# Retention attention and an ELU feed-forward layer on one core: attention in 18 items of four 64-token chunks and eight heads, instead of 36 items of two chunks and four heads

## The chip, the cores and the metric

The kernel runs on one core of a Trainium2 chip. The metric is the time of one execution in microseconds (us) on the device; lower is better. The engines are named as in the profile: PE (TensorE), DVE (VectorE), ACT (ScalarE), POOL (GpSimd) and SP (SyncE, which issues most transfers).

## The reference: what is computed

```python
scores = scale * np.matmul(q, k.transpose(0, 1, 3, 2))      # q, k, v: 8 batches, 8 heads, 576 tokens, 64
gamma = 1.0 - 2.0 ** (-5.0 - np.arange(H, dtype=np.float32))
Dmat = np.where(rel >= 0, gamma[:, None, None] ** rel[None, :, :], 0.0)
x = np.matmul(scores * Dmat, v)                             # then heads side by side: 4608 x 512
h = x @ w_in                                                # 512 -> 2048
g = np.where(h > 0.0, h, np.exp(np.minimum(h, 0.0)) - 1.0)
out = g @ w_out                                             # 2048 -> 512
```

There is no softmax, so the decay is put into q and k beforehand, and attention over earlier tokens can go through a running 64x64 state per head (the sum of k times v) instead of through scores.

## The kernel before, in words

**The plan.** The kernel's operations are objects (`Op`, line 22) with a cost per engine, dependencies, a rank, and the buffers they take and use. `Plan.run` (line 66) goes through a modelled time and gives each engine the ready operation of lowest rank that finds its buffers free. This fixes, once and for all, the order of the instructions of every engine; the chip then runs each engine's list in that order, with waits where data or a buffer is not there yet. Buffers come from `SLOTS` (line 202): `f` are six PSUM banks for everything that PE writes, `sc` one pair of banks for the scores alone.

**Attention before.** An item (36 of them, list `ORDER`) is a main item, 256 tokens of one batch and four heads, or a tail, the last 64 tokens of two batches for eight heads. For each:

- SP loads q, k and v (`load_main`, line 349: 256 KB each; `load_tail`, line 377). POOL and DVE scale q and k into bf16 (`scaled`, line 421; instructions at line 427), POOL or ACT casts v (line 443). q and k are transposed, on PE for the first seven items (`turn_pe`, line 448), by a transposing DMA from SP afterwards (line 491).
- A main item has two chunks of 128 tokens; even and odd tokens are interleaved, so a chunk lies on 64 partitions. `do_scores` (line 547) makes 16 matmuls of 128 columns on 64x64 tiles of PE. DVE multiplies them with the causal mask (line 673, 128x1024). `do_values` (line 585) makes 16 more of 128 columns, `do_state` (line 605) 16 of 64 columns for the sums of k times v per chunk. `do_inter` (line 570) multiplies q with the running states: 128x128 weights, two matmuls of 128 columns per chunk that has a state before it.
- `after_state` (line 619) adds the sums on DVE (lines 630 to 639) and spreads each state to a block-diagonal matrix with a product with `diag` (line 647, mostly POOL). `put_x` (line 696) copies x into the tile `xt` (bf16), two copies of 128x256 per item.
- `stretch(prev, it)` (line 738) is one piece of PE's list: inter of the item before, scores of this item, values of the item before, states of this item. It takes two `f` banks. The first five items are in smaller pieces (`early`, line 772).

**FFN before.** A block is 256 tokens (18 blocks). `ffn1` (line 801) fills one bank with two groups of four matmuls of 256 columns; ACT takes exp (line 817), ACT or DVE does the middle step (lines 827 to 831), DVE joins both into g (lines 839, 841). `ffn2` (line 853) makes a 128x512 output tile with 16 matmuls of 512 columns, in runs of two or four; ACT or DVE copies it out (line 872), SP stores it (line 880). POOL issues the loads of w_in (line 406) and w_out (line 414), four of 512 KB each, at places tied to named operations (`WG`, `WOG`).

All matmuls go through the helper `mm` (line 245), so the profile gives that line for all and the tiles tell them apart: `f<-xt,w_in_sb` is FFN1, `f<-w_out_sb,g` FFN2, `sc<-qkT` scores, `f<-pt,vn` values, `f<-vn,qkn` states, `f<-qkT,s_mid` and `f<-qkT,s_end` inter.

Of the kernel before, what the change touches and what calls it, by code (L numbers as in the profile page):

```python
# [22 lines left out]
class Op:  # L23


    def __init__(self, name, cost, deps, emit, rank, take=(), use=(), banks=(), dma=None, after=None):
        self.name, self.cost, self.emit, self.rank = name, cost, emit, rank
        self.deps = [d for d in deps if d is not None]
        self.turn = [] if after is None else [after]
        self.take, self.use, self.banks, self.dma = take, [*use, *(t[1] for t in take)], banks, dma  # L30
        self.eng = self.start = self.end = self.done = None
        self.slot, self.waits = {}, []


class Plan:
# [30 lines left out]
    def run(self, began):  # L66
# [29 lines left out]
        def pick(e, now):  # L96
            best = None
            for op in ready[e]:
                if best is not None and best[0] <= op.rank:
                    continue  # L100
# [12 lines left out]
                if got is not None:  # L113
                    best = op.rank, op, got
            return best
# [5 lines left out]
        for e, t in began.items():  # L121
            heapq.heappush(events, (t, next(count), None))
        now = 0.0
# [62 lines left out]
ENTER, LEAVE = 1.25, 0.55  # L186


LEAD = 64
HOLD = {}  # L190
RANKS = {}
TOGETHER = 1
EARLY = 5
LOOSE = True
LASTB = 15
ORDER = (0, 1, 2, "t0", 3, "t1", 4, 5, 6, "t2", 7, "t3")
PE_TURN = 7
WG = ("ck11", "ck11", "ck11", "ck12")
WOG = ("ck13", "ck13", "ck13", "ck13")
# [11 lines left out]
def kernel(  # L211
# [15 lines left out]
    FT = 4  # L227
    ST = 64
    NU = FT + 1
    KJ = DM // P  # L230
    NFT = DF // P
    TB = 256
    NP = NFT // 2
    MID = S // 2
    C = 64
    assert (DM, S, D, HP) == (H * D, FT * P + ST, 64, KJ)
# [20 lines left out]
    for h in range(H):  # L257
        nc.vector.memset(lgt[:, h : h + 1], lg[h])
    pos_i = const.tile([P, NU], I32, name="pos_i")
    nc.gpsimd.iota(pos_i[:, :FT].rearrange("p (t e) -> p t e", e=2), pattern=[[2 * P, 2], [1, 2]], base=-MID,  # L260
                   channel_multiplier=2)
    nc.gpsimd.iota(pos_i[:ST, FT:], pattern=[[0, 1]], base=FT * P - MID, channel_multiplier=1)
    nc.gpsimd.iota(pos_i[ST:, FT:], pattern=[[0, 1]], base=MID - FT * P, channel_multiplier=-1)
    pos = const.tile([P, NU], FP32, name="pos")
# [5 lines left out]
    bt = const.tile([P, 1], FP32, name="bt")  # L270
    nc.vector.memset(bt[:ST], math.log(scale))
    nc.vector.memset(bt[ST:], 0.0)
    expo = const.tile([P, NU, H], FP32, name="expo")
    nc.vector.tensor_tensor(
        expo,
        pos.unsqueeze(2).to_broadcast([P, NU, H]),
        lgt.unsqueeze(1).to_broadcast([P, NU, H]),
        ALU.mult,
    )
    gq = const.tile([P, NU, H], FP32, name="gq")  # L280
    nc.scalar.activation(gq[:, :FT], expo[:, :FT], AF.Exp, bias=bq)
    nc.scalar.activation(gq[:, FT], expo[:, FT], AF.Exp, bias=bt)
    gk = const.tile([P, FT, H], FP32, name="gk")
    nc.scalar.activation(gk, expo[:, :FT], AF.Exp, bias=bk, scale=-1.0)

    mask = const.tile([P, 2, 2, C], BF16, name="mask")
    nc.vector.memset(mask, 1.0)
    for c in range(2):
        for ek in range(2):
            for eq in range(2):  # L290
                m = mask[c * C : (c + 1) * C, ek, eq]
                nc.gpsimd.affine_select(out=m, in_=m, compare_op=ALU.is_ge, fill=0.0, base=eq - ek,
                                        pattern=[[2, C]], channel_multiplier=-2)
    mask_t = const.tile([P, ST], BF16, name="mask_t")
    nc.vector.memset(mask_t, 1.0)
    for c in range(2):
        m = mask_t[c * ST : (c + 1) * ST]
        nc.gpsimd.affine_select(out=m, in_=m, compare_op=ALU.is_ge, fill=0.0, base=0, pattern=[[1, ST]],
                                channel_multiplier=-1)
    diag = const.tile([P, 2], FP32, name="diag")  # L300
    nc.gpsimd.memset(diag, 0.0)
    nc.gpsimd.memset(diag[:D, :1], 1.0)
    nc.gpsimd.memset(diag[D:, 1:], 1.0)
# [3 lines left out]

    plan = Plan(SLOTS)  # L310
# [8 lines left out]
    holds, chain = [], {}  # L319
# [4 lines left out]
    items = []  # L324
    for b in ORDER:
        for r in range(FT if isinstance(b, int) else 1):
            it = Item()
            it.tail = not isinstance(b, int)
            if it.tail:
                it.half = int(b[1]) % 2  # L330
                it.b, it.blk = 2 * int(b[1]), "AB"[int(b[1]) // 2]
            else:
                it.b, it.T, it.w = b, r // 2, r % 2
                it.blk = 2 * b + it.T
            items.append(it)
    for n, it in enumerate(items):
        it.n = n
        it.early = n < FT
    at = {(it.b, it.T, it.w): it for it in items if not it.tail}

    seq = list(range(2 * B))
    seq = [*seq[:B], "A", *seq[B:LASTB], "B", *seq[LASTB:]]
    place = {blk: i for i, blk in enumerate(seq)}
    for it in items:
        it.rank = it.n * 4 - 64 if it.early else place[it.blk] * 16 - LEAD + 6 * (it.half if it.tail else it.w)

    def load_main(it, srcs="qkv"):
        n = it.n  # L350
        if not hasattr(it, "ld"):
            it.ld = {}
        for s in srcs:
            src = {"q": q, "k": k, "v": v}[s]
            key, cls = (("rv", n), "rv") if s == "v" else (("rq" + s, n), "rqk")

            def emit(op, src=src, key=key):
                dst = tiles[key].rearrange("p h e d -> p h (e d)")
                pin(nc.sync.dma_start(
                    dst,  # L360
                    src[it.b, 4 * it.w : 4 * it.w + 4, 2 * P * it.T : 2 * P * (it.T + 1), :].rearrange(
                        "h (p e) d -> p h (e d)", e=2),
                ))

            take, use, held = [T(cls, key, [P, 4, 2, D], FP32)], [], []
            if s == "q" and n in HOLD:
                def emit_hold(op, key=key):
# [5 lines left out]
            it.ld[s] = add(f"ld{s}{n}", {"SP": 0.46}, held, emit, len(plan.ops), take=take, use=use,  # L373
                           dma=(0.9 if n or s != "v" else 1.8, 32), after=chain.get(0))
            chain[0] = it.ld[s]

    def load_tail(it):
        n = it.n
        it.ld = {}
        for j in range(2):  # L380
            for i, src in enumerate((q, k)):
                def emit(op, j=j, i=i, src=src):
                    pin(nc.sync.dma_start(tiles["rqt", n, j][i * ST : (i + 1) * ST],
                                          src[it.b + j, :, FT * P :, :].rearrange("h p d -> p h d")))

                it.ld[i, j] = add(f"ldt{i}{j}{n}", {"SP": 0.46}, [], emit, len(plan.ops),
                                  take=[T("rqt", ("rqt", n, j), [P, H, D], FP32)] if i == 0 else [],
                                  use=[] if i == 0 else [("rqt", n, j)], dma=(0.8, 32), after=chain.get(0))
                chain[0] = it.ld[i, j]
        for j in range(2):  # L390
            def emit(op, j=j):
                pin(nc.sync.dma_start(tiles["rvt", n][j * ST : (j + 1) * ST],
                                      v[it.b + j, :, FT * P :, :].rearrange("h p d -> p h d")))

            it.ld["v", j] = add(f"ldt2{j}{n}", {"SP": 0.46}, [], emit, len(plan.ops),
                                take=[T("rvt", ("rvt", n), [P, H, D], FP32)] if j == 0 else [],
                                use=[] if j == 0 else [("rvt", n)], dma=(0.8, 32), after=chain.get(0))
            chain[0] = it.ld["v", j]
# [3 lines left out]
    def load_w_in(n0, n1, after):  # L402
        c = slice(n0 * 512, n1 * 512)
# [4 lines left out]
        op = add(f"wi{n0}", {"POOL": 0.8}, [], emit, -1000, dma=(2.75 * (n1 - n0), 32 * (n1 - n0), 4.9), after=after)  # L408
        for n in range(n0, n1):
            w_in_ld[n] = op  # L410

    def load_w_out(n, after):
        def emit(op):
            pin(nc.gpsimd.dma_start(w_out_sb[:, 4 * n : 4 * n + 4],
# [6 lines left out]
    def scaled(it, i, e, cost):  # L421
# [4 lines left out]
        def emit(op):  # L426
            pin(alu[op.eng].tensor_tensor(tiles[key][:, i, e], tiles[raw][:, :, e], g, ALU.mult))  # L427
# [566 lines left out]
```

## Time and profile before

| what | value |
|---|---|
| three runs | 310.29, 311.6 (median), 312.34 us |
| profiled execution: span from first to last instruction | 307.9 us |
| what lies around the span (median less span; the profile gives no time of its own beyond the span) | 3.7 us |
| PE, DVE, ACT, POOL busy | 294.6, 218.0, 153.4, 148.3 us |
| instructions | 8903 |
| FFN1 matmuls (128x256) | 1152 |
| moved by DMA | 50.12 MB, 163 GB/s over the span |

Times in the profile are microseconds from the first instruction, and a group's line gives its engine, source line, operation, output and input tiles, shape and count. A matmul's duration runs from its start to its modelled end and overlaps its neighbours, so what it costs on PE is read from start to start. Slices are fortieths of the span. A line of waits gives the engine and tile that waited, who released it, and the total time, the number of waits and the longest one.

### The profile page before, as it was taken

How to read it: one execution, taken by the hardware profiler on the slowest of the kernel's cores; microseconds unless marked ns; L12 is line 12 of the kernel's file. 1: busy time of each engine (PE TensorE's matmuls, PEld its weight loads, DVE VectorE, ACT ScalarE, POOL GpSimd, SP SyncE). 2: the span in 40 equal slices, each digit the busy share in tenths (PEclk: the TensorE clock that was granted, in tenths of full speed). 3: DMA queues.
4: the chain of work that ended last, by engine and by line, in shares of the span. 5: the costliest groups of instructions: out<-in, count | busy, mean ns of one | idle time of the engine just before them, and what ended most of it. 6: DMA issues, size and time to landing. Idle time of an engine off the chain costs nothing.

```text
span 307.9 us, 8903 instructions
## 1 busy us (share of the span) xinstructions
PE 294.6 (96%) x3600; PEld 207.0 (67%) x3647; DVE 218.0 (71%) x395; ACT 153.4 (50%) x297; POOL 148.3 (48%) x258
## 2 busy tenths in 40 slices
PE   7789999999999999999999999999999999999995
PEld 3576747767677676676676676667776666666654
DVE  4997835887687878888778787667676666666650
ACT  3467815565556645554545545345446343444431
POOL 5983469958876779988776775003011000000000
PEclk9999999999999999999999999999999999999999
DMA  6999999999999999999999998101011010000122
GB/s 198 271 216 216 216 270 256 263 249 211 247 231 211 217 247 277 243 247 305 247 214 212 274 221 151 36 35 38 34 36 36 35 36 34 36 34 34 39 56 78
DMA packets 103768, 50.12 MB, mean 163 GB/s; under 512 B 45744, under 2 KB 99248, under 8 KB 103728
## 3 DMA queue, kind: packets, MB, share of 16 engines
q1 hardware_dynamic: 99504, 45.37, 69.9%
q0 software_dynamic: 4224, 4.19, 8.0%
q8 instruction: 28, 0.46, 0.6%
q14 instruction: 12, 0.10, 0.1%
HBM read 36.70 MB, written 9.44 MB: 150 GB/s over the span
## 4 chain that ended last, share of the span: by engine, by line
PE 86%; DMA 10%; issue 2%; DVE 1%; POOL 1%; ACT 0%
PE f L245 81%; DMA rqk<-in_q_dram 6%; DMA rqk<-in_k_dram 4%; PE sc L245 3%; PE f L455 1%; POOL qkn L427 0%; PE f L953 0%; DVE qkT L461 0%; POOL s_end L647 0%; DVE qkn L427 0%; ACT ot L872 0%; DVE s_end L647 0%; DVE zero L250 0%; DVE end L639 0%
## 5 line engine op out<-in xcount | busy, mean ns | idle before, releaser
L245 PE MATMUL f<-xt,w_in_sb 128*128 128x256 bf16 x1152 | 147.5, 273 | 0.1
L245 PE MATMUL f<-w_out_sb,g 128*128 128x512 bf16 (+1 forms) x546 | 138.0, 373 | 4.3 <-issue 3.0
L817 ACT ACTIVATE e<-f 128x512 f32<-128x512 f32 x144 | 86.0, 597 | 109.2 <-PE f L245 107.5
L245 PEld LDWEIGHTS <-w_in_sb 128*128 128x128 bf16 x1152 | 111.5, 98 | 38.0
L831 DVE TENSOR_SCALAR em<-e 128x512 bf16<-128x512 f32 x105 | 53.3, 508 | 49.9 <-ACT e L817 49.3
L245 PEld LDWEIGHTS <-g 128*128 128x128 bf16 x592 | 56.0, 98 | 39.4
L841 DVE SCALAR_TENSOR_TENSOR g<-f,em 128x512 bf16<-128x512 f32 x105 | 72.2, 688 | 9.1 <-DVE em L831 0.5
L647 POOL TENSOR_TENSOR s_mid<-mid,diag 128x256 bf16<-128x256 f32 x32 | 20.0, 624 | 51.2 <-ACT mid L630 24.6
L427 POOL TENSOR_TENSOR qkn<-rqk,gq 128x256 bf16<-128x256 f32 x61 | 37.6, 632 | 11.6 <-DMA rqk<-in_q_dram 7.6
L427 POOL TENSOR_TENSOR qkn<-rqk,gk 128x256 bf16<-128x256 f32 x59 | 38.4, 667 | 5.3 <-DMA rqk<-in_k_dram 5.1
L673 DVE TENSOR_TENSOR pt<-sc,mask 128x1024 bf16<-128x1024 f32 x32 | 38.9, 1215 | 1.7 <-PE sc L245 1.7
L839 DVE SCALAR_TENSOR_TENSOR g<-e,f 128x512 bf16<-128x512 f32 x39 | 26.1, 682 | 6.0 <-ACT f L827 6.0
L872 ACT COPY ot<-f 128x512 f32<-128x512 f32 (+1 forms) x36 | 20.6, 575 | 17.8 <-PE f L245 17.7
L708 ACT CAST xt<-f 128x256 bf16<-128x256 f32 x50 | 20.0, 450 | 10.8 <-PE f L245 10.2
L827 ACT ACTIVATE f<-f 128x512 f32<-128x512 f32 x36 | 21.4, 595 | 0.0
L443 POOL CAST vn<-rv 128x512 bf16<-128x512 f32 x28 | 17.6, 629 | 7.4 <-DMA rv<-in_v_dram 7.3
L647 POOL TENSOR_TENSOR s_end<-end,diag 128x256 bf16<-128x256 f32 x28 | 17.4, 623 | 4.2 <-DVE end L639 2.7
L245 PE MATMUL sc<-qkT 64*64 64x128 bf16 x512 | 13.4, 222 | 1.7 <-DVE qkT L461 1.6
L245 PE MATMUL f<-pt,vn 64*64 64x128 bf16 x512 | 12.7, 217 | 0.0
L245 PEld LDWEIGHTS <-qkT 64*64 64x64 bf16 x512 | 8.2, 106 | 5.4 <-DVE qkT L461 2.2
L506 POOL TENSOR_TENSOR qkt<-rqt,gq 128x256 bf16<-128x256 f32 x16 | 9.9, 638 | 3.0 <-DMA rqt<-in_k_dram 3.0
L461 DVE COPY qkT<-f 128x512 bf16<-128x512 bf16 x11 | 4.6, 421 | 9.4 <-PE f L455 9.4
(65 smaller groups left out, 139.4 us busy)
## 6 DMA issues: line engine op xcount, KB each, us to landing
rqk<-in_q_dram SPq DMA_DIRECT2D x32, 256.0 KB, 5.1
rqk<-in_k_dram SPq DMA_DIRECT2D x32, 256.0 KB, 5.2
rv<-in_v_dram SPq DMA_DIRECT2D x32, 256.0 KB, 5.0
out_dram<-ot SPq DMA_DIRECT2D x31, 256.0 KB, 3.7
w_in_sb<-in_moe_w_in_dram POOLq DMA_DIRECT2D x4, 512.0 KB, 12.6
w_out_sb<-in_moe_w_out_dram POOLq DMA_DIRECT2D x4, 512.0 KB, 19.3
out_dram<-ot SPq DMA_DIRECT2D x10, 128.0 KB, 2.4
rqt<-in_q_dram SPq DMA_DIRECT2D x8, 128.0 KB, 4.0
```

The costliest lines, as they stand in the source:

```text
L245: pin(nc.tensor.matmul(*a, **kw))
L427: pin(alu[op.eng].tensor_tensor(tiles[key][:, i, e], tiles[raw][:, :, e], g, ALU.mult))
L443: pin(copy[op.eng](tiles["vn", n], tiles["rv", n]))
L647: pin(alu[op.eng].tensor_tensor(tiles[key].rearrange("p h (j d) -> p h j d", j=2), tiles[src].unsqueeze(2).to_broadcast([P, 2, 2, D]), dia ...
L673: pin(nc.vector.tensor_tensor(tiles["pt", n].rearrange("p i h n -> p (i h) n"), tiles["sc", n].rearrange("p i (h n) -> p (i h) n", h=2), m ...
L708: pin(copy[op.eng](dst, src))
L817: pin(nc.scalar.activation(tiles[ekey], tiles[hkey], AF.Exp))
L827: pin(nc.scalar.activation(ph, ph, AF.Relu))
L831: pin(alu[op.eng].tensor_scalar_add(em, e, -1.0))
L839: pin(nc.vector.scalar_tensor_tensor(g, e, -1.0, ph, ALU.add, ALU.min))
L841: pin(nc.vector.scalar_tensor_tensor(g, ph, 0.0, tiles["em", blk, p], ALU.max, ALU.min))
L872: pin(copy[op.eng](tiles[okey][:, :width], tiles[pkey][:, :width]))
```

## The change

Attention goes in 18 items (`ATT`) of all eight heads: 16 of 256 tokens of a batch, and two of the last 64 tokens of four batches ("X", "Y"). Each has four chunks of 64 tokens, and with even and odd tokens interleaved a chunk lies on 32 partitions. Scores use 64x32 tiles of PE (64 matmuls of 64 columns an item), values and states 32x64 tiles (64 of 64 columns each), inter 128x128 weights and four matmuls of 64 columns per chunk that has a state. A state is kept per chunk: four sums on DVE or ACT, and two copies of half the partitions into a standing zeroed block-diagonal tile (`ring`) on POOL, ACT or DVE, in place of the product with `diag`. The mask is two DVE products of 128x512 per item.

PSUM is one pool of eight banks. A stretch takes six together: two for scores, four for x (columns 0 to 255) and the new states (columns 256 to 511). A test in the plan (`gate`) decides when the plan begins to collect those six banks.

FFN goes in 11 blocks: four of 256 tokens, seven of 512. For the latter FFN1's matmuls have 512 columns, four to a bank. Two items, not five, are in small pieces at the start; four, not seven, are transposed on PE; weights come in five pieces (256, 256, 512, 512, 512 KB) for w_in and four for w_out, not before given times of the plan (`AT`). The rank lead of attention over FFN (`LEAD`) is 96 for 64. In the built program PE has 1152 score, 1152 value, 1024 state and 256 inter matmuls, 64 transposes, 256 FFN1 matmuls of 256 columns and 448 of 512.

```diff
-    "f": 6, "sc": 1,
-    "rqk": 8, "rv": 8, "qkn": 5, "vn": 6, "qkT": 5, "pt": 3,
-    "rqt": 4, "rvt": 2, "qkt": 4, "vt": 2, "qkTt": 4, "ptt": 2,
-    "xt": 5, "g": 20, "e": 4, "em": 4, "ot": 5, "mid": 4, "end": 4, "s_mid": 4, "s_end": 16,
+    "f": 8, "rq": 3, "rk": 3, "rv": 3, "qkn": 3, "vn": 3, "qkT": 3, "pt": 2,
+    "xt": 4, "g": 33, "e": 4, "em": 4, "ot": 5, "S": 6,
...
-LEAD = 64
+LEAD = 96
+EARLY = 2
+PE_TURN = 4
+AT = {"wi0": 9.6, "wi1": 10.4, "wi2": 11.2, "wi3": 13.0, "wi4": 15.0, "wo0": 17.0, "wo1": 19.0, "wo2": 22.0, "wo3": 25.0}
+ATT = ((0, 0), (0, 1), (1, 0), (1, 1), (2, 0), (2, 1), (3, 0), (3, 1), (4, 0), (4, 1), "X",
+       (5, 0), (5, 1), (6, 0), (6, 1), (7, 0), (7, 1), "Y")
+FFN = (((0, 0),), ((0, 1),), ((1, 0),), ((1, 1),), ((2, 0), (2, 1)), ((3, 0), (3, 1)), ((4, 0), (4, 1)),
+       ((5, 0), (5, 1)), ((6, 0), (6, 1)), ("X", "Y"), ((7, 0), (7, 1)))
...
     def do_scores(it):
-        for hl in range(2):
-            for ek in range(2):
-                for i in range(2):
-                    r = slice(i * D, (i + 1) * D)
-                    for c in range(2):
-                        cs = slice(c * C, (c + 1) * C)
-                        o = (hl * 2 + ek) * P
-                        mm(pairs(sc[cs, i, o : o + P]), tt[r, 4 + ek * 2 + hl, cs], queries(n, r, hl, c),
-                           start=True, stop=True)
+        tt = tiles["qkT", it.n]
+        for hp in range(HP):
+            for ek in range(2):
+                for c in range(NC):
+                    for i in range(2):
+                        part = slice(i * D, (i + 1) * D)
+                        sc = tiles["sc", it.n, i].rearrange("p (h k n) -> p h k n", h=HP, k=2)
+                        mm(pairs(sc[rows(c), hp, ek]), tt[part, 1, ek, hp, rows(c)], queries(it, part, hp, c),
+                           start=True, stop=True)
...
+    def do_inter(it, xkey):
+        for c in range(NC):
+            s = state_of(it, c)
+            if s is not None:
+                for hp in range(HP):
+                    acc((xkey, c), 2, pairs(tiles[xkey, c][:, hp * C : (hp + 1) * C]), tiles[s][:, hp],
+                        queries(it, slice(0, P), hp, c))
+
+    def do_values(it, xkey):
+        vn, pt = tiles["vn", it.n], tiles["pt", it.n]
+        for hp in range(HP):
+            for ek in range(2):
+                for c in range(NC):
+                    for i in range(2):
+                        acc((xkey, c), i, tiles[xkey, c][i * D : (i + 1) * D, hp * C : (hp + 1) * C],
+                            vn[rows(c), 2 * hp + i, ek], pt[rows(c), i, hp, ek])
...
+            def emit_s(op, skey=skey, prev=prev, st_ap=st_ap):
+                if prev is None:
+                    pin(copy[op.eng](tiles[skey], st_ap()))
+                else:
+                    pin(nc.vector.tensor_tensor(tiles[skey], st_ap(), tiles[prev[1]], ALU.add))
...
+            def emit_b(op, skey=skey, bkey=bkey):
+                for i in range(2):
+                    part = slice(i * D, (i + 1) * D)
+                    pin(copy[op.eng](tiles[bkey][part, :, part], tiles[skey][part]))
...
     def stretch(prev, it):
...
+        st = add(f"A{it.n if it else 'last'}", {"PE": cost}, deps, emit, (it or prev).rank - 4, use=use)
+        reserve(st, ([("sc", it.n, i) for i in range(2)] if it else []) + banks_of(xkey))
...
     def ffn1
...
-            for f in range(2):
-                ft = 2 * p + f
+            for f, ft in enumerate(fts):
                 for j in range(KJ):
-                    mm(ph[:, f * TB : (f + 1) * TB], w_in_sb[:, j, ft * P : (ft + 1) * P], xt[:, j],
+                    mm(ph[:, f * blk.w : (f + 1) * blk.w], w_in_sb[:, j, ft * P : (ft + 1) * P], xt[:, j],
                        start=(j == 0), stop=(j == KJ - 1))
```

More of the change, by code (lines that the diff above doesn't have):

```diff
@@ L287 @@
+    nc.scalar.activation(gk, expo, AF.Exp, bias=bk, scale=-1.0)
+    mask = const.tile([P, 2, 2, R], BF16, name="mask")
     nc.vector.memset(mask, 1.0)
-    for c in range(2):
+    for c in range(NC):
         for ek in range(2):
[L290 to L303, printed above, removed]
+            m = mask[c * R : (c + 1) * R, ek]
@@ L317, in T @@
         return (cls, key, shape, dt)
-    holds, chain = [], {}
     class Item:
         pass
[L324 to L349, printed above, removed]
-        n = it.n
[L351 to L366, printed above, removed]
+    items, at = [], {}
@@ L367, in emit_hold, with load @@
+    chain, holds = {}, []
+    def load(it):
+        n = it.n
+        it.ld = {}
+        for s, src in (("q", q), ("k", k), ("v", v)):
+            key, cls = ("r" + s, n), "r" + s
+            take, use, held = [T(cls, key, [P, H, 2, D], FP32)], [], []
+            if n in HOLD and s == "q":
                 def emit_hold(op, key=key):
@@ L372, in load_main @@
                 take, use = [], [key]
[L373 to L398, printed above, removed]
@@ new lines, in prepare, with emit @@
+        for hs in halves:
+            def emit(op, hs=hs):
+                pin(copy[op.eng](tiles[vkey][:, hs], tiles["rv", n][:, hs]))
+            vfirst = not it.cv
+            it.cv.append(add(f"cv{hs.start}_{n}", {"ACT": 0.62, "POOL": 0.64, "DVE": (0.42, 0.3)} if it.early else
+                             {"POOL": 0.64, "ACT": (0.62, 1.0)}, lds(it, "v", hs), emit, it.rank,
+                             take=[T("vn", vkey, [P, H, 2, D], BF16)] if vfirst else [],
+                             use=[("rv", n)] + ([] if vfirst else [vkey]), after=None if vfirst else it.cv[0]))
@@ new lines, in rows, with queries, pairs @@
+    def rows(c):
+        return slice(c * R, (c + 1) * R)
+    def queries(it, part, hp, c):
+        return tiles["qkT", it.n][part, 0, :, hp, rows(c)]
+    def pairs(ap):
+        return ap.rearrange("p (e r) -> p e r", e=2)
+    def do_scores(it):
+        tt = tiles["qkT", it.n]
[7 more added lines that the diff above has]
+                           start=True, stop=True)
@@ L746, in stretch @@
         if it is not None:
[L747 to L751 removed]
+            deps += [*it.turned, *it.cv]
+            use += [("qkT", it.n)] + ([] if it.tail else [("qkn", it.n), ("vn", it.n)])
+            cost += cost_of(it, "s" if it.tail else "st")
         def emit(op):
@@ L853, in ffn2, with rows_of @@
-    def ffn2(blk, it, c, per, rank, n0=0, n1=DM):
-        pkey, okey = ("p", blk, it, n0), ("ot", blk, it, n0)
-        nfp, width = per // 2, n1 - n0
+                pin(nc.vector.scalar_tensor_tensor(g, ph, 0.0, tiles[mkey], ALU.max, ALU.min))
+        blk.g[p] = add(f"g_{blk.i}_{p}", {"DVE": 0.69}, [md], emit_g, rank, take=[T("g", gkey, [P, 512], BF16)],
+                       use=[hkey, ekey, mkey], banks=[(hkey, 0)])
+        return f1
+    def rows_of(blk, t):
+        it, half = blk.its[t // 2], t % 2
+        if not it.tail:
+            return [(0, P, it.b * S + it.T * TB + half * P)]
+        return [(j * C, C, (it.b + 2 * half + j) * S + 2 * TB) for j in range(2)]
```

691 lines of the change are left out of this document (316 added, 375 removed).

## The prediction, on record before the changed kernel ran

> **What bounds the kernel now.** I read the page's busy times first, then the waits of TensorE (PE) after the start, then the timeline of PE.
>
> ```profile
> PE 294.6 (96%) x3600; PEld 207.0 (67%) x3647; DVE 218.0 (71%) x395; ACT 153.4 (50%) x297; POOL 148.3 (48%) x258
> PEclk9999999999999999999999999999999999999999
> DMA  6999999999999999999999998101011010000122
> PE 86%; DMA 10%; issue 2%; DVE 1%; POOL 1%; ACT 0%
> ```
>
> PE is busy 96% of the 307.9 us at full granted clock, and the chain that ends last is PE for 86%. DMA is busy in nine tenths of every slice up to about 185 us, and 10% of the chain is DMA: that is the start. From 48 to 305 us the waits of PE are this one line:
>
> ```profile
> PE f L245 <- issue: 3.0, 19, 0.2
> ```
>
> 19 waits of 0.16 us, each in front of an "x3" of FFN2 where the code issues four: a matmul without a record. So PE never waits once the kernel runs, and the time after the start is the sum of what PE issues. What one thing costs on PE is not its mean duration (matmuls overlap) but the step from one start to the next:
>
> ```profile
> 49.81 3.66 PE L245 MATMUL f<-xt,w_in_sb 128*128 128x256 bf16 x32
> 53.31 1.03 PE L245 MATMUL f<-w_out_sb,g 128*128 128x512 bf16 x4
> 54.17 1.04 PE L245 MATMUL f<-xt,w_in_sb 128*128 128x256 bf16 x8
> ...
> 55.91 0.27 PE L245 MATMUL f<-qkT,s_end 128*128 128x128 bf16 x2
> 56.02 0.28 PE L245 MATMUL f<-qkT,s_mid 128*128 128x128 bf16 x2
> 56.22 0.42 PE L245 MATMUL sc<-qkT 64*64 64x128 bf16 x16
> 56.47 0.39 PE L245 MATMUL f<-pt,vn 64*64 64x128 bf16 x16
> 56.70 0.29 PE L245 MATMUL f<-vn,qkn 64*64 64x64 bf16 x16
> 56.92 1.05 PE L245 MATMUL f<-xt,w_in_sb 128*128 128x256 bf16 x8
> ...
> 81.10 0.32 PE L245 MATMUL sc<-qkTt 64*64 64x64 bf16 x16
> 81.25 0.40 PE L245 MATMUL f<-pt,vn 64*64 64x128 bf16 x16
> ```
>
> To be seen: 32 FFN1 matmuls of 256 columns take 53.31 - 49.81 = 3.50 us (109 ns each), four FFN2 matmuls of 512 columns 0.86 us (216 ns each). One attention stretch (states into x, scores, values, new states) takes 56.92 - 55.91 = 1.01 us: four 128-column matmuls at 56 ns, a change of tile shape, 16 + 16 + 16 small ones, a change back. Sixteen scores of 64 columns take 0.15 us. In the single records four 64x64 tiles start 3.3 ns apart and run side by side; the next four follow 56 ns later at 128 columns and 32 ns later at 64. A change of shape costs 0.09 to 0.10 us beyond the normal step (last inter start 62.31, first score 62.46; the step is 0.056).
>
> FFN needs 1152 x 0.109 + 576 x 0.216 = 250.0 us of the span whatever the attention does; the rest, 58 us, is start, attention and end (3.4 us from the last matmul to the end).
>
> **The change part by part.**
>
> Attention before: of 32 main items, 16 have four inter matmuls (1.01 us) and 16 have two (0.90 us): 30.7 us. Four tails at about 0.6 us (8 inter at 29 ns, scores 0.15, values 0.13, shape change 0.1): 2.4 us. Together 33.1 us. After: 18 items for all 8 heads. Inter: 16 matmuls of 64 columns at the 29 ns that the tails' form shows (12 for a first block). Scores, values, states: 64 matmuls each, eight tiles side by side. The trace has no 64x32 or 32x64 tile. Bounds: eight side by side at the 32 ns of a 64-column group make 8 x 0.032 = 0.25 us for 64; only four side by side, as the rows show, make 0.51 us. I take 0.25, because a tile of the new shape is half of one that the rows show and every eight consecutive matmuls name eight different tiles. There is one more shape change, since scores and values now differ. A second block: 0.46 + 0.09 + 0.25 + 0.09 + 0.25 + 0.25 + 0.10 = 1.49 us; a first one 1.38; a tail 1.24. 8 x 1.49 + 8 x 1.38 + 2 x 1.24 = 25.4 us. Term: -7.7 us.
>
> FFN1: seven of eleven blocks are 512 tokens wide, 448 matmuls at the 216 ns of the 512-column row in place of 896 at 109: 448 x (0.216 - 0.218) = -0.9 us.
>
> Start: the first FFN1 stands at 18.76 us, after w_in, whose loads are issued from 9.29 us and take 8.5 us at least for 512 KB. After, the first two pieces are 256 KB and follow POOL's four scalings, as in before; the landing is between the 5 us of a 256 KB load on SP's queue and those 8.5 us, and I take 7.5 (near its own kind), so the first FFN1 about 17.3: -1.5 us (between -4 and 0). Against it PE has 64 transposes for 56 and eight groups of them, not six, behind the first FFN1, each 0.25 us, each possibly late behind a load as they are in before (waits of 0.2 to 1.0 us there): +1.0 us (0 to +4). q, k and v of an item come as six loads of 256 KB in either kernel, so SP's queue gives the first items no earlier.
>
> PSUM banks: scores have no banks of their own any more. A stretch takes six of eight banks (two for scores, four for x and states), so FFN has two until VectorE and ScalarE have emptied them. Lower end 0, the row above. Upper end: the last FFN1 bank ahead of a stretch needs exp 0.60, relu 0.60, g 0.69 and hops, 2.2 us, while the order puts one FFN2 run of 0.86 us behind it: 1.3 us late x 16 stretches = 21 us. In the middle of the order the FFN1 bank before that has 2.6 us, and two banks may stay in use, so I stay near the lower end: +2 us.
>
> VectorE: 36 masks of 0.69 for 32 of 1.215 and four of 0.68: -16.8 us. 56 state sums of 128x256 at about 0.42 (the 128x256 copy's row) for 51 of 0.28: +9.3 us. FFN's chains are the same 144 of 512. It stays off the path, as do POOL (124 half-height block copies, 100 of them on POOL, for 64 block products of 0.62; the scalings are half as many and twice as wide) and ACT. Their cover is FFN on PE; if it is gone, POOL's 148 us over the first 190 show how little room there is: the next things late would be the block copies, and with them the inter matmuls at the head of a stretch. On SP the transposing DMAs are 28 wide for 25 wide and 8 half ones, tail loads take rows of 512 B for 256 B: 0.
>
> Sum: -7.7 - 0.9 - 1.5 + 1.0 + 2.0 = -7.1 us. The span goes from 307.9 to 300.8. The median of the three runs, 311.6, lies 3.7 us over the span, which I leave as it is: **304.5 us**, 2.3% faster.
>
> **The rivals.**
>
> Issue of small matmuls (slower). A full stretch was 52 pairs of load and matmul and becomes 208. How fast PE is fed matters only once its queue is empty: its closing drain is on record at 302.40 us with exactly 16 loads still to start, so 16 pairs are queued. The densest place of the trace has 47 loads within 457 ns from 86.25 us; less the 16 queued, 31 pairs in 457 ns, so a pair takes at most 14.7 ns. It takes at least the 3.3 ns between neighbours. Behind the inter matmuls 176 pairs must come in 0.95 us. At 14.7 ns they take 2.59 us: +1.64 us x 16 stretches = 26 us, about 331 us. The gain of 7 us is gone from 8 ns per pair on (176 x 8.1 = 1.42 us, +0.47 x 16). For it: nothing in before asked for more than 52 pairs in a row. Against it: no start in those bursts is late, up to the last group.
>
> [...]
>
> Four tiles, not eight, at once (the change does not do what it says): 0.25 us more in each of 52 groups of 64, 13 us, 317 us. For it: no such row. Against: the four tiles of before never hinder each other.
>
> Banks: 0.5 us per stretch rather than 0.13, 6 us more, 310.5 us. For it: six banks at once. Against: no bank wait in before, where a stretch held four.
>
> Loads late: the last stretch has 104 us of FFN behind it (its matmuls in the order at the steps above), in before 68 us, so attention ends 36 us earlier, about when the loads ended in before (DMA drops after 185 us). Transposing DMAs stand at least 6.2 us ahead of their scores in before and land in 4.9: 1.3 us of room. If DMA delivers no faster than its mean of 240 GB/s, a stretch late by 5 us costs 5 us, since PE's order is fixed: 309.5 us.
>
> **How the numbers follow.** Forecast, 300 to 308 us by its own bounds: 0.50. Better, through a start 5 us shorter and no bank waits (297.5): 0.07. Issue: 0.18, half of it mild (8 to 9 ns a pair, 311 to 317), half worse. The 25 ns rule: 0.02. Four tiles: 0.05. Banks: 0.11. Loads late: 0.07. Three runs of this kernel spread by 0.7%, so about 1% is what a measurement tells from no change. Faster by over 1% (below 308.5): the forecast, the better case and half of banks and loads late, 0.66. Within 1%: the other half and some mild issue, 0.14. Slower: 0.20. The range leaves out about 0.1 at each end: 298 to 317 us.
>
> **What would show it.** Right: 64 scores in a row from start to start within 0.27 us, a full stretch of 1.5 us, FFN1 at 216 ns per 512 columns, no PE wait after 50 us over 0.3 us, first FFN1 near 17 us. Wrong: 64 small matmuls taking 0.4 us or more with even steps (issue) or with groups of four (tiles); PE waits on ACT or DVE ahead of a stretch (banks) or on a transposing DMA or POOL (loads); a VectorE over 80% busy.

## The result, and the profile after

The changed kernel takes 371.51 us (median of five runs, 368.33 to 372.76): 1.191 times the kernel before, 95% interval 1.186 to 1.197. I had said 304.5 us, and 317 at most. Ratios, here and below, are from runs counted as fast (at most 1.5% above the fastest of the same kernel), against the kernel before as it ran in the same batch (medians 310.24 to 311.6 us).

The page of the changed kernel: busy time, the granted clock by slices, the queue that brings instructions, and the shares of the chain that ended last.

```profile
span 366.4 us, 11811 instructions
PE 323.2 (88%) x5066; PEld 186.4 (51%) x5097; DVE 213.4 (58%) x402; ACT 167.1 (46%) x329; POOL 142.7 (39%) x239
PEclk9788999699989989989999889699999999999999
q8 instruction: 40, 0.66, 0.8%
PE 84%; issue 11%; POOL 2%; DMA 1%; ACT 1%; DVE 1%; SPq 0%; POOLq 0%; ACTq 0%
```

PE's busy share fell from 96 to 88%, the clock is below nine tenths in a quarter of the slices (for none before), and 11% of the chain is "issue": PE stood still and nothing that the profile shows held it. The waits of PE (total, number, longest) say the same:

```profile
PE f L252 <- issue: 31.9, 26, 3.8
PE f L866 <- issue: 3.6, 1, 3.6
PE f L252 <- DVE zero L257: 1.3, 1, 1.3
```

After the start no wait on a bank, a load or a copy is over 0.8 us; 35 us are waits for nothing. The timeline of TensorE (PE) shows where:

```profile
60.53 1.03 PE L252 MATMUL f<-w_out_sb,g 128*128 128x512 bf16 x4
61.39 0.51 PE L252 MATMUL f<-qkT,bd 128*128 128x64 bf16 x12
61.84 0.68 PE L252 MATMUL f<-qkT 64*32 64x64 bf16 x64
62.45 0.70 PE L252 MATMUL f<-pt,vn 32*64 32x64 bf16 x64
62.95 0.57 PE L252 MATMUL f<-vn,qkn 32*64 32x64 bf16 x41
66.64 0.39 PE L252 MATMUL f<-vn,qkn 32*64 32x64 bf16 x23 [3.12 <-issue]
67.36 3.19 PE L252 MATMUL f<-w_out_sb,g 128*128 128x512 bf16 x7 [0.33 <-issue]
70.35 8.10 PE L252 MATMUL f<-xt,w_in_sb 128*128 128x256 bf16 x64
```

Three things are to be seen. Scores take 62.45 - 61.84 = 0.61 us up to the first value, where I had 0.34 (0.25 and a change of shape of 0.09). In the middle of the states, whose data are all there, PE stands still for 3.1 us. And the seven FFN2 matmuls behind it take 2.99 us to the next start, 427 ns each instead of 216: half the clock.

From the single records, the 58.5 us by which the span grew, by the steps between weight loads: pauses (steps over 0.6 us) 37.2 us in 15 places, for 3.4 before: +33.8; the rest of FFN 258.9 us for 245.8: +13.1, of which 51 steps of 380 to 440 ns are some 10; the rest of attention 51.1 us for 46.7: +4.4; fillers at the start 14.2 for 7.0: +7.2.

The pauses have an address. The built program has 10212 instructions on PE (7296 before), and 0.66 MB in 40 packets are 16 KB each. That makes 64.2 bytes for an instruction (62.9 in the kernel before, which has 28 packets), so I take 64, and 256 of them in a packet. Nearly all the long pauses stand where the place in PE's program is 194 or 195 modulo 256, which I take for the place between the last instruction of one packet and the first of the next: after each of the 15 PE goes on 1.1 to 1.6 us behind the end of a packet. (In the records all 15 stand 91 to 96 pairs behind a multiple of 128; the count slips because some records are missing.)

### The profile page after: what moved, and what is told of

It reads as the page before. It is cut to its first block, busy times and chain, and to the rows that moved or that the text cites. A ratio compares the mean times of both kernels' runs of the same rounds, so it can differ in the third digit from the quotient of the medians.

```text
span 366.4 us, 11811 instructions
## 1 busy us (share of the span) xinstructions
PE 323.2 (88%) x5066; PEld 186.4 (51%) x5097; DVE 213.4 (58%) x402; ACT 167.1 (46%) x329; POOL 142.7 (39%) x239
## 4 chain that ended last, share of the span: by engine, by line
PE 84%; issue 11%; POOL 2%; DMA 1%; ACT 1%; DVE 1%; SPq 0%; POOLq 0%; ACTq 0%
PE f L252 82%; DMA rk<-in_k_dram 1%; PE f L459 1%; POOL bd L582 1%; POOL qkn L427 1%; PE f L866 0%; ACT e L723 0%; DVE em L737 0%; ACT qkT L468 0%; SPq L368 0%; DVE g L747 0%; DVE g L745 0%; ACT f L733 0%; ACT S L563 0%; ACT ot L784 0%
## 5 line engine op out<-in xcount | busy, mean ns | idle before, releaser
L252 PE MATMUL f<-xt,w_in_sb 128*128 128x512 bf16 (+1 forms) x694 | 150.6, 359 | 1.8 <-ACT e L723 0.8
L252 PEld LDWEIGHTS <-w_in_sb 128*128 128x128 bf16 x704 | 71.4, 103 | 63.2 <-issue 11.0
L582 POOL CAST bd<-S 64x256 bf16<-64x256 f32 x100 | 41.3, 413 | 95.1 <-DVE S L565 54.4
L427 POOL TENSOR_TENSOR qkn<-rq,gq 128x512 bf16<-128x512 f32 (+1 forms) x38 | 36.0, 963 | 4.7 <-DMA rq<-in_q_dram 3.8
L427 POOL TENSOR_TENSOR qkn<-rk,gk 128x512 bf16<-128x512 f32 (+1 forms) x39 | 36.8, 961 | 1.1 <-DMA rk<-in_k_dram 0.4
L252 PE MATMUL f<-vn,qkn 32*64 32x64 bf16 x1024 | 13.9, 207 | 25.1 <-issue 25.1
L593 DVE TENSOR_TENSOR pt<-f,mask 128x512 bf16<-128x512 f32 x36 | 24.2, 685 | 13.4 <-PE f L252 13.3
L565 DVE TENSOR_TENSOR S<-f,S 128x256 f32<-128x256 f32 x56 | 23.5, 420 | 5.8 <-ACT S L563 1.5
L252 PE MATMUL f<-qkT 64*32 64x64 bf16 x1152 | 12.5, 195 | 3.8 <-issue 3.8
L252 PE MATMUL f<-pt,vn 32*64 32x64 bf16 x1152 | 13.3, 204 | 0.7 <-issue 0.7
```

Of the source, the lines that this page charges most:

```text
L252: pin(nc.tensor.matmul(*a, **kw))
L427: pin(alu[op.eng].tensor_tensor(tiles[key][:, i, e, hs], tiles["r" + s, n][:, hs, e], g, ALU.mult))
L565: pin(nc.vector.tensor_tensor(tiles[skey], st_ap(), tiles[prev[1]], ALU.add))
L582: pin(copy[op.eng](tiles[bkey][part, :, part], tiles[skey][part]))
L593: pin(nc.vector.tensor_tensor(tiles["pt", n][:, i].rearrange("p h k n -> p h (k n)"), tiles["sc", n, i].rearrange("p (h n) -> p h n", h=HP ...
```

## The experiments

**Fetch theory**: PE runs through a block of 256 instructions (128 pairs of weight load and matmul) faster than the next block comes, and halts at the border. Rivals: the **shape** theory (the new tile shapes stop PE now and then), the **banks** theory (six PSUM banks at a time), and issue rate alone (even steps, no pauses).

### Stretch cut in three pieces, 1.7 and 2.6 us between them

```diff
-            cost += cost_of(prev, "iv")
+            cost += cost_of(prev, "i")
...
+            nxt = add(f"B{name}", {"PE": 0.45 + cost_of(prev, "v")}, inter_deps(prev), lambda op: do_values(prev, xkey), rank,
+                      use=banks_of(xkey) + inter_uses(prev), after=st)
+            st.follow = st = nxt          # not before GAP us after the piece ahead: 1.7, in the other kernel 2.6
```

(states likewise as a third piece.)

> The changed kernel with each stretch cut into three pieces on PE (inter and scores; values; states) with about 1.7 us of FFN between them; same matmuls, same banks, same transfers. Theory F (fetch): PE's instructions come in blocks of 256 (one 16 KB packet each); a block is asked for when the one before it is entered and takes 2.5 to 4.7 us, and a stretch of 416 instructions uses up a block in 1.1 us. Then the waits over 0.7 us (15 of them, 37 us) shrink to under 8 us, the granted clock goes from 0.943 to over 0.98, and the time falls by 37 + 11 less what is left: about 325 us (315 to 338). Theory S (shape): 64x32 and 32x64 tiles themselves stop PE; the same matmuls give the same waits, 360 us or more. Theory B (banks): six banks are held 3.5 us longer, so waits grow, over 375 us.

> The same cut with about 2.6 us of FFN between the pieces. F: the gap covers more of the fetch, waits under 5 us in all, 318 to 332 us, at most a few us from the 1.7 us version. S: 360 us or more. B: worse than the 1.7 us version.

Measured: 340.97 us (ratio 1.098, 1.094 to 1.101) and 343.38 us (1.105, 1.100 to 1.110). Pauses: 17.0 us in 10 places and 17.5 in 9. With FFN between the pieces half of the pauses are gone, with the same small matmuls on the same tiles and banks. This alone doesn't prove that the gap did it, since the cut also moves every later instruction (the last experiment shows what that does). Both are slower than I expected of fetch alone, with pauses of 17 us where I had said under 8 and under 5; the wider gap brought nothing more. Of split17's pauses 7.9 us are the two at 11.9 and 24.0 us, in the start, which no gap reaches.

### The kernel before, with its small matmuls cut by columns

Old tile shapes, old items, each small matmul in two or four parts, so 100 or 196 pairs a stretch for 52:

```diff
-                        o = (hl * 2 + ek) * P
-                        mm(pairs(sc[cs, i, o : o + P]), tt[r, 4 + ek * 2 + hl, cs], queries(n, r, hl, c),
-                           start=True, stop=True)
+                            o = (hl * 2 + ek) * P + part * w          # w = P // 4, in the other kernel P // 2
+                            eq, q0 = divmod(part * w, C)
+                            mm(sc[cs, i, o : o + w], tt[r, 4 + ek * 2 + hl, cs],
+                               tt[r, eq * 2 + hl, c * C + q0 : c * C + q0 + w], start=True, stop=True)
```

(values and states likewise.)

> The kernel before, with each score, value and state matmul of the main items cut by columns into four (32, 32 and 16 columns), still on 64x64 tiles; 196 pairs of load and matmul per stretch in place of 52, same arithmetic, same banks. F: waits of 1 to 4 us inside the stretches as in the changed kernel, in over half of the 31 stretches (40 us or more), clock under 0.97, and 8.3 ns a pair (+0.9 us per stretch, 28 us): 365 to 410 us. S: no such waits, since the shape is the old one: at most 16 groups of four at 32 ns per phase, +0.8 us per stretch, under 340 us.

> The same cut into two (64, 64 and 32 columns): 100 pairs, 200 instructions per stretch, fewer than a block. F: two block borders seldom fall into one stretch, waits under 10 us in all, 8.3 ns a pair bind only the last part: 314 to 328 us, far from half of what the cut into four costs. S: 312 to 322 us, no waits.

Measured: 419.82 us in four parts (1.353, 1.342 to 1.363), 321.27 in two (1.035, 1.030 to 1.040). The former went past my upper bound of 410. The waits of PE with four parts:

```profile
PE f L245 <- issue: 47.4, 41, 3.9
PE sc L245 <- issue: 8.6, 3, 4.6
```

Pauses: 58.3 us in 25 places with four parts, 6.5 in 4 with two, all four before 27 us (the kernel before has four there too, 3.4 us). Of the 25, 23 stand at a border of blocks, counted as above. The 64x64 tiles of before halt as well, with two f banks a stretch, and the pauses go with the number of instructions (58.3 us at 196 pairs a stretch, 6.5 at 100). Shape and banks fall.

### Bursts by themselves

A program without the reference's work: 1536 pairs with idle DMA queues, the same with 24 loads in flight, then short bursts between large matmuls.

```diff
+    def small(n):
+        for m in range(n // 8):
+            for c in range(4):
+                for i in range(2):
+                    r, o = slice(32 * c, 32 * c + 32), slice(64 * i, 64 * i + 64)
+                    pin(nc.tensor.matmul(bank[c][o, :64], lhs[r, o], rhs[r, :64], start=True, stop=True))
```

> A program that computes none of the reference, on the same chip: 40 large matmuls (128 x 512), then 1536 pairs of a 32x64 weight load and a 64-column matmul, each pair on another of the eight tiles, with the DMA queues idle; then the same 1536 pairs with 24 loads of 256 KB in flight; then three times five short runs of 64, 128, 192, 256 and 384 such pairs with 26 large matmuls (5.6 us) ahead of each, the DMA idle again. Fetch theory: a block of 256 instructions is 128 pairs. Within a block pairs follow each other at 8 to 9 ns (1.1 us a block); at the borders TensorE stands still, so that a block takes as long as the fetch of one: 2 to 3 us with idle DMA, 3 to 4.5 us while the loads run, and 1536 pairs take 24 to 36 us and 36 to 55 us instead of 13. Short runs: no pause over 0.7 us in those of 64 pairs, pauses in those of 256 and 384 (1 and 2 each). The shape theory (small tiles themselves stop TensorE now and then) has pauses that don't fall 128 pairs apart and that don't get longer with loads in flight. The issue theory alone has even steps of 8 ns and no pause.

The timeline of this program: first the long burst with idle DMA, then part of the one with loads, then a round of short bursts (64, 128, 192, 256 pairs).

```profile
13.14 1.70 PE L45 MATMUL bank<-rhs,lhs 32*64 32x64 bf16 x183
17.05 1.29 PE L45 MATMUL bank<-rhs,lhs 32*64 32x64 bf16 x128 [2.22 <-issue]
20.78 1.35 PE L45 MATMUL bank<-rhs,lhs 32*64 32x64 bf16 x128 [2.43 <-issue]
...
70.73 1.36 PE L45 MATMUL bank<-rhs,lhs 32*64 32x64 bf16 x128 [3.52 <-issue]
75.28 1.36 PE L45 MATMUL bank<-rhs,lhs 32*64 32x64 bf16 x128 [3.19 <-issue]
...
117.63 0.71 PE L45 MATMUL bank<-rhs,lhs 32*64 32x64 bf16 x64
118.27 5.78 PE L38 MATMUL wide<-rhs,lhs 128*128 128x512 bf16 x26
123.98 1.24 PE L45 MATMUL bank<-rhs,lhs 32*64 32x64 bf16 x128
125.16 5.79 PE L38 MATMUL wide<-rhs,lhs 128*128 128x512 bf16 x26
130.87 1.77 PE L45 MATMUL bank<-rhs,lhs 32*64 32x64 bf16 x192
132.58 5.79 PE L38 MATMUL wide<-rhs,lhs 128*128 128x512 bf16 x26
138.29 1.65 PE L45 MATMUL bank<-rhs,lhs 32*64 32x64 bf16 x177
142.65 0.83 PE L45 MATMUL bank<-rhs,lhs 32*64 32x64 bf16 x79 [2.71 <-issue]
143.41 7.47 PE L38 MATMUL wide<-rhs,lhs 128*128 128x512 bf16 x26
```

The transfers in the first burst (13 to 57 us), with nothing else on the queues:

```profile
DMA packets 12, 0.20 MB, mean 4 GB/s; under 512 B 0, under 2 KB 0, under 8 KB 0
q8 instruction: 12, 0.20, 2.1%
```

After the second border of each long burst PE stops after exactly 128 pairs, every time (22 pauses in all, of 2.3 to 3.7 us from one weight load to the next), and a packet comes for each stop (12 packets for the 11 stops of the idle burst). From border to border it takes 3.73 or 4.00 us in the burst with idle queues and 4.55 and 4.83 while the loads run (70.73 to 75.28 to 80.11); the loads are through at 82.4 us, and after the block of 4.00 us that holds that moment it takes 3.45 or 3.73. The pairs themselves take 1.1 us of it. In the single records of the idle burst a packet starts 1.0 to 1.7 us after the block before it was entered, moves for 0.9 to 1.5 us, and PE goes on 1.3 to 1.6 us after its end. So I take one block to be ahead and no more; of the 3.73 or 4.00 us of a block, 0.9 to 1.5 go on moving its packet. Bursts of 64, 128 and 192 pairs never pause, those of 256 once, of 384 twice, in each of three rounds (which stand at nearly the same places against the borders). The 192 hold two borders; the first lies 12 pairs in, and the packet that it asks for starts at 128.89 us, 2.0 us ahead of the matmul at that border, which fits some 30 pairs queued ahead of PE (the steps of 3.3 ns below).

Fetch is right in all that it said, except that a block takes longer than my 2 to 3 us: the idle burst took 43 us, not 24 to 36. Steps without pauses are as in the kernel: some 30 pairs 3.3 ns apart, eight tiles side by side, then even steps of 8.3 ns. And large matmuls after such a pause are slower: 26 take 7.47 us after one of 2.7 us, 5.79 without, as seven took 427 ns each in the changed kernel.

### FFN1 on 256 tokens again, attention's part alone

```diff
-FFN = (((0, 0),), ((0, 1),), ((1, 0),), ((1, 1),), ((2, 0), (2, 1)), ((3, 0), (3, 1)), ((4, 0), (4, 1)),
-       ((5, 0), (5, 1)), ((6, 0), (6, 1)), ("X", "Y"), ((7, 0), (7, 1)))
+FFN = (((0, 0),), ((0, 1),), ((1, 0),), ((1, 1),), ((2, 0),), ((2, 1),), ((3, 0),), ((3, 1),), ((4, 0),), ((4, 1),),
+       ((5, 0),), ((5, 1),), ((6, 0),), ((6, 1),), ("X",), ((7, 0),), ((7, 1),), ("Y",))
...
-    "xt": 4, "g": 33, "e": 4, "em": 4, "ot": 5, "S": 6,
+    "xt": 8, "g": 33, "e": 4, "em": 4, "ot": 5, "S": 6,
```

> The changed kernel with every FFN block on 256 tokens again (18 blocks; 8 xt buffers of half the size in place of 4), so that attention's part of the change is left alone. Fetch theory: the bursts of small pairs are the same and so are their pauses; FFN1 goes by 512 more pairs of 109 ns in place of 512 fewer of 216 (about 1 us more), 3 more packets of instructions: 366 to 380 us, near the 371.5 of the changed kernel. If FFN1 on 512 tokens had a part in the loss (its blocks come in twos and ask for two items at a time), this is faster: under 360.

Measured: 369.86 us (1.190, 1.186 to 1.194), pauses 36.2 us in 15 places. The loss is there without the wide FFN1. A few us either way can't be read from this pair, since the edit also moves the bursts against the borders.

### The first load of w_in in two, in the kernel before

```diff
-    for n in range(4):
-        load_w_in(n, n + 1, None)
+    for n in ((0, 1), (1, 2), (2, 4), (4, 6), (6, 8)):      # in units of 256 columns
+        load_w_in(*n, None)
```

> The kernel before with one part of the change alone: the first load of w_in cut in two of 256 columns each, so that the first FFN1 unit waits for 256 KB in place of 512 KB. My forecast gave 1.5 us for this (first FFN1 at 17.3 us in place of 18.76). No theory of the loss says anything against it: ratio 0.995 (0.990 to 1.001). If one more issue on GpSimd's queue (0.8 us) delays the casts behind it, it is 1.000 to 1.005.

Measured: 311.34 us, ratio 1.0024 (1.0000 to 1.0049): no gain, where I had expected 0.995. The timeline of PE in this kernel:

```profile
16.23 1.04 PE L245 MATMUL f<-xt,w_in_sb 128*128 128x256 bf16 x8
...
18.38 1.03 PE L245 MATMUL f<-xt,w_in_sb 128*128 128x256 bf16 x8
...
21.77 1.05 PE L245 MATMUL f<-xt,w_in_sb 128*128 128x256 bf16 x8 [1.05 <-DMA w_in_sb<-in_moe_w_in_dram]
```

The first FFN1 does come 2.5 us earlier (16.23 for 18.76), but the next w_in piece is not there until 21.77, so what is gained is waited for again.

### Fewer fillers, and the last cut of the stretch

The changed kernel fills PE's idle time before 50 us with zero matmuls of 128 columns. (In its trace nothing but zero matmuls has run on PE when the granted clock goes to full at 4.0 us: those of 512 columns take 427 ns before it, 216 after.) Here the fillers have 512, a quarter as many: 156 instructions fewer, all in the start. split34 is the stretch in three with 3.4 us between; split34f has both.

```diff
-                    for _ in range(int(gap * 0.8 / 0.06)):
-                        mm(spot[:, :P], zero[:, :P], zero[:, :P], start=True, stop=True)
+                    for _ in range(int(gap * 0.8 / 0.22)):
+                        mm(spot, zero[:, :P], zero, start=True, stop=True)
```

> The changed kernel with the fillers ahead of 50 us (zero matmuls that keep TensorE's clock up while the first items come in) 512 columns wide again in place of 128, a quarter as many: 156 instructions fewer in the first 30 us; the filler transposes stay. Fetch theory: the two pauses of 3.8 and 4.0 us in the first 30 us come from blocks run through by fillers and small pairs faster than they can be fetched; with fewer fillers at least one of them shrinks by half or more, and the time falls by 2 to 8 us: 363 to 369 us. If those pauses are something else of the start (late tiles, the half clock), nothing changes: 370 to 373.

> The stretch in three pieces as in the first two split kernels, with 3.4 us planned between them. By the measured 3.7 to 4.8 us a block, no block is left within less than its fetch after the first 30 us: pauses over 0.6 us fall from 17 us in all (10 of them at the start) to 8 to 11. But the pieces hold a stretch for 9 us, so waits of other kinds may grow. Fetch theory with the even issue rate (8 ns a pair): 332 to 342 us, still 20 us or more above the kernel before, since without the pauses attention is no shorter than before. If the pauses were all that is wrong with the small tiles, it would be 318 to 325.

> split34 and the wide fillers together. Fetch theory: both gains add: 326 to 338 us, with the pauses at the start down to 2 to 6 us. If under 305, small tiles without pauses would beat the kernel before, as I forecast for the change; I give that little, since even steps of 8 ns take the whole gain.

Measured: 338.43 us for the wide fillers (1.092, 1.085 to 1.100), 339.57 for split34 (1.095, 1.089 to 1.102), 337.66 for both (1.085, 1.078 to 1.092). The two gains do not add: 33, 32 and 34 us. The first is a miss that matters: 33 us better, not 2 to 8. The waits of PE with wide fillers:

```profile
PE f L252 <- issue: 12.6, 8, 3.9
```

The pauses fell from 37.2 to 15.5 us, most of that long after 50 us, where not one instruction differs. Either the start has an effect that lasts, or it is the place of each burst against the borders, which moved by 156. So I followed each program's order through, small pairs at 8.6 ns, others by their columns, a block to be had 3.7 us after the one ahead was entered. It gives 36 us of pauses in 16 places for the changed kernel (its trace 37 in 15), 16 in 8 with wide fillers (15.5 in 9), 30 in 13 with FFN1 on 256 tokens (36 in 15), 56 in 26 for four column parts (58 in 25), 3 in 3 for two (6.5 in 4). For the kernels in three pieces it gives 3.5 to 5 us where the traces have 12 to 17, so it isn't all there. Part of the difference is not fetch at all. With both changes (split34f) the waits of PE for nothing are down to 3.9 us; the others are for copies and sums of the pieces themselves, as I had feared of split34:

```profile
PE f L257 <- issue: 3.9, 3, 2.2
PE f L257 <- POOL bd L587: 2.0, 3, 0.8
PE f L257 <- ACT xt L622: 1.7, 1, 1.7
```

In split17, though, 13 of the 17 us stand at borders, and why the calculation gives less is open.

### The same work, moved against the borders

```diff
                 elif spot is not None:
+                    for _ in range(56 if op.start < 3 else 0):      # 52 in the kernel with wide fillers
+                        mm(spot[:D, :D], zero[:R, :D], zero[:R, :D], start=True, stop=True)
```

> The changed kernel, nothing taken away: 56 more pairs of the smallest kind (32x64 tiles on zeros, 8.6 ns each, 0.5 us in all) ahead of the first filler, so that every later instruction of TensorE stands 112 places further on against the borders of the 256-instruction blocks. Fetch theory: a burst of 416 instructions pauses when two borders fall into it. Following the program order through, with a block to be had no earlier than 3.73 us (the measured pace of the burst program) after the one before it was entered, the changed kernel has 16 pauses of 36 us in all (its trace has 15 of 37), and with this shift 8 of 14 us. So it gets faster by more work: 335 to 350 us, near the 338 of the kernel with wide fillers. If the 33 us that the wide fillers gave came from the start itself (less work, a fuller clock there), this is 371 to 374.

> The opposite shift: the kernel with wide fillers (338.4 us; the same way of counting gives it 8 pauses of 16 us, its trace has 9 of 15.5) with 52 such small pairs ahead of its first filler, 104 places. Fetch theory: 17 pauses of 39 us, and the gain of the wide fillers is gone: 362 to 376 us. If the wide fillers themselves were the gain, 338 to 341.

Measured: the changed kernel with 56 small pairs more takes 342.83 us (1.101, 1.096 to 1.106), 29 less; the one with wide fillers and 52 pairs more takes 382.52 us (1.230, 1.224 to 1.236), 44 more. First the waits of PE of the former, then of the latter:

```profile
PE f L252 <- issue: 18.6, 22, 3.9
```

```profile
PE f L252 <- issue: 41.9, 34, 3.6
```

Half a microsecond of added work takes 29 us off or puts 44 on, and the pauses in the records go with it: 21.3 us in 12 places, and 41.1 in 15 (worked out beforehand: 14 in 8, 39 in 17). The second went past my upper bound of 376. Of the theories here only the borders explain this: TensorE's work behind the first filler is the same in each of the two pairs of kernels, and all 15 pauses of the latter kernel and 11 of the former's 12 stand at a border.

## Why the prediction was wrong

**The step that failed** is the attention term, -7.7 us, and in it "64 = 8 x 0.032 = 0.25 us". Eight tiles do run side by side, as I took it (3.3 ns from start to start, groups of eight), but only for some 30 pairs at the head of the scores, and again at the head of the values, behind the change of shape. After that pairs come every 8.3 ns, and 64 scores or values take 0.48 or 0.49 us from the first start to the last. A stretch without a pause, with wide fillers, is this:

```profile
108.40 0.51 PE L252 MATMUL f<-qkT,bd 128*128 128x64 bf16 x12
108.85 0.68 PE L252 MATMUL f<-qkT 64*32 64x64 bf16 x64
109.46 0.71 PE L252 MATMUL f<-pt,vn 32*64 32x64 bf16 x64
109.97 0.89 PE L252 MATMUL f<-vn,qkn 32*64 32x64 bf16 x64
110.78 1.47 PE L252 MATMUL f<-xt,w_in_sb 128*128 128x512 bf16 x6
```

110.78 - 108.40 = 2.38 us, where I had 1.38 for a first block. Attention without its pauses costs 51.1 us of steps for 46.7, +4.4 instead of -7.7. That much the issue rival had, pace included: 8 to 9 ns a pair, 311 to 317 us, which I held half of 0.18 likely. I kept it low because 52 pairs in a row showed no late start. But 52 pairs are hardly more than the 30 that start 3.3 ns apart here, and which I take to be queued (I had read 16 from a single drain), so they could not show the sustained pace. The rival's own ceiling, 14.7 ns a pair and 331 us, fell for the same reason: it came from 47 pairs in a row.

**What no part of the prediction had** is the supply of the instructions themselves, which it put at nothing without a reason. It passes over this line of the page of before:

```profile
q8 instruction: 28, 0.46, 0.6%
```

As a share of DMA time that is nothing. What counts is the rate, which no line of before shows and the bursts by themselves do: 256 instructions every 3.7 us, 14 ns each and so 29 ns a pair. The kernel before never asks for more for long: 104 instructions a stretch, then FFN at 109 or 216 ns a pair. The new stretch asks for 416 in about 2.3 us; it holds one border or two, 128 pairs or about 1.1 us apart, and the second comes too early unless large matmuls in the queue cover it, as I read the bursts of 192 pairs behind 26 of them. Pauses: +33.8 us.

**Half clock**: in the trace of the changed kernel the granted clock falls to half in nine spells of 3.4 or 6.8 us, 41 us in all, each beginning in one of the eleven pauses of 1.9 us and more, or at most 1.5 us behind it. Two of these eleven, of 2.7 us at 139.3 and 245.6 us, have no such spell: from 142.77 us seven FFN2 matmuls take 1.51 us, 216 ns each. What decides is not shown. The spells make most of FFN's +13.1 us. The granted clock was 0.943 over the span; with wide fillers 0.968.

**Start**: forecast -1.5 and +1.0. The first FFN1 stands at 22.95 us, not 17.3: a pause of 3.6 us at 11.9 and 26 narrow fillers at half clock (16.00 to 18.77 us) ahead of it. In the kernel before, the earlier load alone brought nothing (1.0024).

**FFN1 on 512 tokens**: -0.9 us forecast, too small to be seen (369.86 us without it, 371.51 with it, ranges overlapping). The step of 216 ns is right (269.64 us for four of 512 columns to the next start at 270.51).

**Banks, loads, POOL, VectorE**: no wait of PE on them after the start beyond 0.8 us. My +2 us for banks was 0.8 at most, and both rivals fell. The four-tiles rival fell by the eight starts 3.3 ns apart. No run shows the "25 ns rule" that has 0.02 among the chances: small matmuls started 3.3 and 8.3 ns apart, and most of the loss is in pauses.

**What stays open**: with pauses down to 11.7 us, of which 3.9 are waits for nothing, the kernel in three pieces with wide fillers is still 27 us behind the one before. The steps of its profiled run, whose span is 24.4 us longer, give +8.3 pauses, +4.5 attention, +5.8 FFN, +5.5 fillers; how much of the last two is clock, I did not separate. Why a block takes 3.7 us when its packet takes 0.9 to 1.5 is not shown either. No version beat the kernel before.

## What to carry to other kernels

Count instructions, not only their durations. The changed kernel, with stretches of 416 instructions (208 pairs) in about 2.3 us, halted 15 times for 0.9 to 4.0 us, nine times with half the clock in or behind it, and all 15 at the same place against the borders of its blocks. A block of 256 instructions (128 pairs) came 3.45 to 4.83 us after the one ahead of it in the bursts by themselves. Bursts there of 192 pairs behind 26 large matmuls never halted, those of 256 always did. Splitting work over more and smaller tiles trades array time for instructions: 208 pairs a stretch for 52 here, and at 8.3 ns a pair attention without its pauses took 51.1 us for 46.7. When times jump by tens of microseconds for an edit somewhere harmless (29 off and 44 on here), look whether the code moved against its block borders before believing in the edit.

## What the runs showed of the hardware that I had not expected

- A block of 256 instructions came 3.45 to 4.00 us after the one ahead of it was entered, with idle queues, and 4.55 and 4.83 us with loads in flight; in each long burst PE stopped after every 128 pairs from the second border on.
- Some 30 small pairs start 3.3 ns apart after a pause or a change of tile shape; beyond that a pair of a small weight load and matmul costs 8.3 ns on 64x32 and 32x64 tiles, and on 64x64 tiles 64 pairs take 0.52 us (four column parts).
- The same work, but for 0.5 us, took 338.4 or 382.5 us by where its bursts lay against the borders.
- Nine of eleven pauses of 1.9 us and more had the granted clock at half for 3.4 or 6.8 us (26 large matmuls 7.47 us for 5.79 behind another); the four shorter ones in the changed kernel's trace had not.
